# Program order on every engine for the first nine pieces of the first block, and a solve one step sooner, in a fused delta-rule attention and maxout kernel

## The chip, the cores and the metric

The kernel runs on one core of one Trainium2 chip. The metric is the device time of one execution in microseconds (us). Engines are called PE (TensorE), ACT (ScalarE), DVE (VectorE), POOL (GpSimd) and SP (SyncE, which issues most of the DMA here). PSUM is the memory in which the kernel's matmul products land. A *hole* is a stretch in which PE stands idle, and *by hand* means in the order of the program. All times and ratios quoted are of runs in the fast state. "L687" is line 687 of the kernel; the lines of all versions shown here agree up to about line 1015.

## The reference, cut to what matters

```python
# q, k, v: (4, 8, 768, 48), beta: (4, 8, 768)
k_n = k / (norm(k) + 1e-6)
for t in range(768):                       # delta rule, state is 48 x 48 per head
    y[t]  = q[t] @ state
    v_old = state.T @ k_n[t]
    state += beta[t] * outer(k_n[t], v[t] - v_old)
x = y as (3072, 384)
out = max(x @ w1, x @ w2, x @ w3) @ w_out  # d_ff = 768
```

The kernel does the attention in 12 chunks of 64 tokens, two chunks to a group. In each group a triangular system is solved (`solve`, many small DVE instructions), its result is multiplied out by matmuls, and the output of a finished group is the input of one block of the maxout network (`ffn`). The six blocks of `ffn` are the frame of the program: each yields after every piece of matmuls, and between two pieces the program emits a bit of the attention of the next group.

## The kernel before

Products of the attention go through one PSUM tag (a set of buffers under one name) with **three** buffers; the maxout products have two of their own:

```python
def ps_ffn(shape, name):
    return psum.tile(shape, FP32, name=name, tag="ffn", bufs=2)

def ps_two(name):                                   # p_k, p_q, p_g, p_t, p_e, ...
    return psum.tile([128, 2, 512], FP32, name=name, tag="two", bufs=3)
```

Those that the argument follows, and what empties their buffers:

```python
def old_k(c):      # link "k": product p_k, emptied by DVE at L687; needs the scaled v_t
    nc.vector.tensor_tensor(out=rhs, in0=rhs, in1=times_state(kqt, 0, "p_k"), op=ALU.subtract)
def old_q(c):      # link "q": product p_q, emptied by ACT at L695
    nc.scalar.copy(heads(qs), times_state(kqt, 1, "p_q"))
# gram ("P", "g"): product p_g, emptied by DVE at L395 (masked product pt) or ACT at L428 (at)
# turn ("T", "t"): transposes p_t, emptied by ACT at L345 (kqt)
# halves_z ("e"): product p_e, emptied by ACT at L614 (z)
```

Work on the same engines that waits for transfers:

```python
def prep_sums(c):
    for g in range(2):
        nc.scalar.square(ksq, kk)                      # L267, needs the key tile kpad
        nc.vector.tensor_reduce(out=..., in_=ksq, ...) # L268
    for bb in range(2):                                # "flip": halves exchanged by DMA
        nc.sync.dma_start(out=ksum[rows(bb), 1], in_=kflip[rows(1 - bb)])   # L273
def prep_values(c):
    norm(...)         # root on ACT (L245), Newton step on DVE (L246 to L250)
    scale(c, nrm)     # v_t on POOL (L277)
def prep(c): prep_sums(c); prep_values(c)              # cut
def weights():        # one piece a step: mant, up on ACT (L211, L220), POOL, DVE, POOL
    ...               # needs w_bits, a staged DMA
```

The first block and the main loop. Within `manual_schedule` an engine keeps the order of the program; engines outside it are ordered by the scheduler. So before piece 4 all engines follow the program, from there only PE does:

```python
for i, _ in enumerate(ffn(0)):
    if i == 4:                                         # the border
        by_hand.close()
        tc.no_sync_barrier()
        by_hand = ExitStack()
        by_hand.enter_context(tc.manual_schedule(engines={mybir.EngineType.PE}))
    if i > 3:
        some(conv, 1)                                  # one conversion of weights
        fetch(nc.sync)
    queries(FIRST.get(i, ""))
    links(1, EARLY_LINKS.get(i, ""))                   # 9: "k0 q0", 10: "e0 t0", ...
    ...
    if i in (8, 9):
        prep(i - 6)
    ...                                                # cut
# main loop: all engines by hand
for m in range(1, GROUPS):
    for i, _ in enumerate(ffn(m)):
        if i < 2: some(solving, 1)                     # steps below: 3, from piece 18 on 4
        if m + 2 < GROUPS:
            if i == 9:  blocks(m + 2)
            if i == 11: solving = solve(m + 2)
        if i > 11: some(solving, steps - 2)
        links(m + 1, LINKS.get(i, ""))   # "d": T1's transposes, "t": turn, "L", "N": loads
        if i >= 11: some(solving, 2)
```

Of the kernel before, what the change touches and what calls it, by code (L numbers as in the profile page):

```python
# [21 lines left out]
def kernel(  # L22
# [81 lines left out]
    def rows(bb):  # L104
        return slice(C * bb, C * (bb + 1))
# [6 lines left out]
    def load(src, dst, n, queues):  # L112
        c, g = divmod(n, 2)
        for bb in range(2):
            queues[bb].dma_start(
                out=dst[rows(bb ^ g), :, 0:D],
                in_=src[2 * bb + g, :, c * C : (c + 1) * C, :].rearrange(
                    "h p d -> p h d"
                ),
            )  # L120

    def load_k(n, queues=one_queue):
        load(k, kpad[n % NK], n, queues)

    def load_q(n, queues=one_queue):
        load(q, qpad[n % NQ], n, queues)

    def load_v(c):
        vts[c] = work.tile([128, 2, H, D], FP32, name="v_t", bufs=3)
        for bb in range(2):  # L130
            nc.sync.dma_start(
                out=vts[c][rows(bb)].rearrange("p g h d -> p (g h) d"),
                in_=v[2 * bb : 2 * bb + 2, :, c * C : (c + 1) * C, :].rearrange(
                    "b h p d -> p (b h) d"
                ),
            )
# [28 lines left out]
    t1 = [const.tile([128, 2, H, BL], FP32, name=f"t1{i}") for i in range(NU)]  # L165
# [22 lines left out]
    def fetch(queue=nc.scalar):  # L188
        if fetched[0] < len(pieces):
            _, src, (a, b) = pieces[fetched[0]]  # L190
            st = work.tile([128, 2 * 384], U32, name="w_bits", bufs=5)
            queue.dma_start(
                out=st.rearrange("p (a b) -> p a b", a=a), in_=src
            )
            staged.append(st)
            fetched[0] += 1
# [46 lines left out]
    def norm(out, ksum, root, t):  # L243

        nc.scalar.sqrt(root, ksum)  # L245
        nc.vector.tensor_scalar_max(t, root, 1e-30)  # L246
        nc.vector.reciprocal(t, t)
        nc.vector.tensor_tensor(out=t, in0=t, in1=ksum, op=ALU.mult)
        nc.vector.tensor_tensor(out=t, in0=t, in1=root, op=ALU.add)
        nc.vector.tensor_scalar(  # L250
            out=out, in0=t, scalar1=0.5, scalar2=1e-6, op0=ALU.mult, op1=ALU.add
        )

    def small(name, *shape):
        one = name[-1] == "0" or name[-2:] == "bl" or name == "warm"
        return work.tile([128, *shape], FP32, name=name, bufs=2 - one)
# [3 lines left out]
    def prep_sums(c):  # L260


        ksum, kflip = small("ksum", 2, H), small("kflip", H)
        for g in range(2):
            kk = kpad[(2 * c + g) % NK][:, :, 0:D]
            ksq = work.tile([128, H, D], FP32, name="ksq", tag="o_sb")
            nc.scalar.square(ksq, kk)  # L267
            nc.vector.tensor_reduce(  # L268
                out=kflip if g else ksum[:, 0], in_=ksq,
                axis=mybir.AxisListType.X, op=ALU.add,  # L270
            )
        for bb in range(2):
            nc.sync.dma_start(out=ksum[rows(bb), 1], in_=kflip[rows(1 - bb)])  # L273
        sums[c] = ksum

    def scale(c, nrm):
        nc.gpsimd.tensor_tensor(  # L277
            out=vts[c], in0=vts[c],
            in1=nrm[:, :, :, None].to_broadcast([128, 2, H, D]), op=ALU.mult,
        )  # L280

    def prep_values(c):

        nrm = small("nrm", 2, H)
        norm(nrm, sums.pop(c), small("root", 2, H), small("newton", 2, H))
        scale(c, nrm)
# [30 lines left out]
    def prep(c):  # L317
        prep_sums(c)
        prep_values(c)
# [38 lines left out]
    def load_blocks(n):  # L358
        c, g = divmod(n, 2)
        for i in range(2):  # L360
            t = turned[n, i] = work.tile(
                [128, 2, TURNED], FP32, name="turned", tag="w_bits", bufs=5
            )
            nc.gpsimd.memset(t[:, :, TURNED - 48 : TURNED], 0.0)  # L364
            for bb in range(2):
                for par in range(2):
                    for db in range(2):
                        p0, at = DP * par + 32 * db, 32 * (1 - db)
                        (nc.sync, nc.gpsimd)[i].dma_start(  # L369
                            out=t[p0 : p0 + 32, bb, at : at + NP * 2 * D].rearrange(  # L370
                                "p (j x) -> p j x", j=NP
                            ),
                            in_=(k, q)[i][
                                2 * bb + g, :, c * C : (c + 1) * C, :
                            ].rearrange(
                                "(j two) (r tb) d -> two r j (tb d)", two=2, tb=2
                            )[par],
                        )
# [483 lines left out]
    def some(gen, n):  # L862
        for _ in range(n):
            if next(gen, gen) is gen:
                break

    conv = weights()
    solving = solve(0)
# [86 lines left out]
    for n in range(2):  # L955
# [4 lines left out]
    solving = solve(1)  # L960
# [3 lines left out]


    LINKS = {
        0: "k0 q0 t0 L2", 1: "g0 t1 L3", 2: "g1 t2", 3: "d0 d1", 4: "z0", 5: "z1 g2",
        6: "j0 t3", 7: "j1 g3", 8: "u0", 9: "s0", 10: "y0", 11: "k1 q1 x0",
        12: "w0 V0", 13: "u1", 14: "K0 K1 V1", 15: "y1 x1 X0", 16: "K2 K3 p0",
        17: "s1 w1 p1", 18: "N0 P0", 19: "X1 P1", 20: "N1",  # L970
    }
    EARLY_LINKS = {
        9: "k0 q0", 10: "e0 t0", 11: "e1 t1", 12: "f0 g0", 13: "f1 d0 g1",
        14: "z0 d1 t2", 15: "z1 g2", 16: "j0 t3", 17: "j1 g3", 18: "u0", 19: "s0",
        20: "k1 q1", 21: "y0", 22: "u1", 23: "x0", 24: "s1", 26: "y1", 28: "x1",
    }


    FIRST = {
        0: "f1 s0 T2 S1 S1", 1: "z1 d1 S1 k1 P2 T3 S1 S1", 2: "j1 S1 S1 S1",  # L980
        3: "P3 S1 q1 S1 S1", 4: "u1 T4", 5: "y1", 6: "s1 T5 P4", 7: "x1 T6",
        8: "P5 T7", 12: "P6", 14: "P7",
    }


# [8 lines left out]
    def links(m, names):  # L994
        for name in names.split():
            f, i = name[0], int(name[1])
            if f in RECURS and m < GROUPS:
                RECURS[f](2 * m + i)
            elif f in MADE and m + 1 < GROUPS:
                MADE[f](2 * (m + 1) + i)  # L1000
            elif f in UNIT and m + 1 < GROUPS:
                UNIT[f](4 * (m + 1) + i)
            elif f == "N" and m + 2 < GROUPS:
                load_blocks(4 * (m + 2) + i)

    def queries(names):
        for name in names.split():
            f, n = name[0], int(name[1])
            if f not in OF_KEYS:
                links(0, name)  # L1010
                continue
            OF_KEYS[f](n)
            if f == "T" and n + 3 < 11:
                load_q(n + 3)
# [1 line left out]


    for i, _ in enumerate(ffn(0)):
        if i == 4:
            by_hand.close()  # L1020
            tc.no_sync_barrier()
            by_hand = ExitStack()
            by_hand.enter_context(tc.manual_schedule(engines={mybir.EngineType.PE}))
        if i > 3:
            some(conv, 1)
            fetch(nc.sync)
        queries(FIRST.get(i, ""))
        links(1, EARLY_LINKS.get(i, ""))
        if 4 <= i < 8:
            some(solving, 2)  # L1030
        if i == 4:
            load_v(3)
        if 5 <= i < 9:
            load_k(3 + i)
        if i in (8, 9):
            prep(i - 6)
        if i == 12:
            load_q(11)
        if i in (15, 18):
            load_v(4 + i // 18)  # L1040
        if i in (18, 20):
            prep(4 + i // 20)
        if i == 19:
            blocks(2)
        if i == 21:
            solving = solve(2)
            some(solving, 1)
        if 21 <= i < 29:
            some(solving, 4)
        if i in (27, 28):  # L1050
            load_blocks(i - 15)
# [8 lines left out]
    for m in range(1, GROUPS):  # L1060
        for i, _ in enumerate(ffn(m)):
            if i < 2:
                some(solving, 1)
            if m + 2 < GROUPS:
                if i == 9:
                    blocks(m + 2)
                if i == 11:
                    solving = solve(m + 2)
            steps = 4 if i >= 18 else 3
            if i > 11:  # L1070
                some(solving, steps - 2)
            links(m + 1, LINKS.get(i, ""))
            if i >= 11:
                some(solving, 2)
    by_hand.close()
# [28 lines left out]
```

## Time and profile before

| | us |
|---|---|
| median time of 3 runs | 599.53 (595.86 to 600.70) |
| profiled span | 596.8 |
| start of the first p_h | 60.2 |
| first block, up to the first p_h of the next | 134.4 |
| blocks 1 to 5 | 82.2, 88.8, 88.9, 76.1, 66.2 |

The block borders are the starts of the first p_h after a run of p_o. The lines of the page and of the blocks are in the prediction below. One stretch that the prediction did not show turned out to matter. It is from the instructions in order of time (start us, us, engine and line, output and inputs, and in brackets the idle time of the engine before it and what ended that):

```profile
103.41 1.15 PE L675 MATMUL p_k<-st,kqt 48*64 48x48 f32 x64
...
106.60 0.80 ACT L695 COPY qs<-p_q 128x768 f32<-128x768 f32 x1 [1.80 <-PE p_q L675]
...
107.97 1.14 PE L611 MATMUL p_e<-ut,at 64*64 64x32 f32 x64
...
126.71 0.94 DVE L687 TENSOR_TENSOR v_t<-v_t,p_k 128x768 f32<-128x768 f32 x1
```

ACT stood ready for p_q and emptied its buffer at once. p_k, in contrast, kept its buffer for more than 22 us, until L687, and PE went on meanwhile with the other two.

### The profile page before, as it was taken

Reading aid. Unit: us, or ns where it says so; the run is one execution under the profiler, and the core shown is the slowest. Engines: PE = TensorE matmul, PEld = TensorE weight load, DVE = VectorE, ACT = ScalarE, POOL = GpSimd, SP = SyncE. Lnnn points to the kernel's source line nnn. Section 1 sums busy time; section 2 is a strip of 40 time slices with the busy share of each in tenths; the row PEclk is TensorE's granted clock in tenths of the full one; section 3 lists DMA queues with packets and bytes.
Section 4 is the critical chain, followed back from the end, with each engine's and each line's share of the span. In section 5 each row is a group of like instructions: output and inputs, shape, how many; then the busy total and the mean of one; then the engine's idle time right before and its main releaser. Section 6 shows DMA issues by size and latency. Waiting matters only on the chain.

```text
span 596.8 us, 18730 instructions
## 1 busy us (share of the span) xinstructions
PE 547.5 (92%) x8106; PEld 322.4 (54%) x8106; DVE 343.4 (58%) x778; ACT 139.8 (23%) x274; POOL 119.7 (20%) x209
## 2 busy tenths in 40 slices
PE   5467888978999999999979999979999999999997
PEld 4346766765556545555435555545555455554444
DVE  1658886696399463899363899363898422211110
ACT  3336246555111221121111212111211111010000
POOL 6024224258210512005602005600001000000000
PEclk9555698988999999999979999979999999999999
DMA  9999739754701654454734654733653202210002
GB/s 159 162 169 243 147 71 184 192 142 104 121 17 26 145 115 82 98 117 110 170 86 82 116 99 106 178 83 57 121 103 74 42 2 55 61 45 1 0 0 53
DMA packets 159505, 58.76 MB, mean 98 GB/s; under 512 B 141184, under 2 KB 153280, under 8 KB 159424
## 3 DMA queue, kind: packets, MB, share of 16 engines
q1 hardware_dynamic: 150736, 51.58, 41.4%
q0 software_dynamic: 3200, 4.82, 3.6%
q10 hardware_dynamic: 5488, 1.18, 1.2%
q8 instruction: 63, 1.03, 0.8%
q14 instruction: 18, 0.15, 0.1%
HBM read 40.21 MB, written 17.30 MB: 96 GB/s over the span
## 4 chain that ended last, share of the span: by engine, by line
PE 69%; DVE 4%; SPq 2%; issue 1%; DMA 1%; ACT 0%; POOL 0%; DVEq 0%; POOLq 0%; ACTq 0%
PE p_h L822 42%; PE p_o L846 16%; PE p_g L411 2%; PE p_u L703 2%; PE p_y L743 2%; PE p_k L675 2%; PE p_s L725 1%; PE p_q L675 1%; SPq L369 1%; PE p_j L658 1%; DVE tmp L519 1%; DMA turned<-in_k_dram 1%; DVE y_bl L523 1%; SPq L537 0%; DVE h L832 0%
## 5 line engine op out<-in xcount | busy, mean ns | idle before, releaser
L822 PE MATMUL p_h<-xt,w_sb 128*128 128x512 f32 (+1 forms) x702 | 308.2, 585 | 5.8 <-DVE h L832 4.2
L822 PEld LDWEIGHTS p_h<-xt,w_sb 128*128 128x128 f32 x702 | 132.6, 198 | 130.1 <-issue 114.6
L832 DVE TENSOR_TENSOR h<-h,p_h 128x512 f32<-128x512 f32 (+1 forms) x78 | 50.2, 644 | 100.7 <-PE p_h L822 100.4
L846 PE MATMUL p_o<-wo_sb,h 128*128 128x384 f32 x288 | 94.4, 487 | 0.6 <-DVE h L832 0.6
L846 PEld LDWEIGHTS p_o<-wo_sb,h 128*128 128x128 f32 x288 | 54.3, 190 | 38.1 <-issue 1.7
L277 POOL TENSOR_TENSOR v_t<-v_t,nrm 128x768 f32<-128x768 f32 x12 | 17.9, 1491 | 204.0 <-DVE nrm L250 129.9
L523 DVE TENSOR_TENSOR y_bl<-y_bl,tmp 128x31 f32<-128x31 f32 (+20 forms) x139 | 53.3, 384 | 4.7
L369 POOL DMA_DIRECT2D turned<-in_q_dram x96 | 52.2, 551 | 3.1 <-POOL turned L364 3.1
L519 DVE TENSOR_TENSOR tmp<-x_bl,y_bl 128x31 f32<-128x31 f32 (+20 forms) x139 | 47.1, 339 | 4.1
L830 ACT COPY h<-p_h 128x512 f32<-128x512 f32 (+1 forms) x39 | 21.5, 552 | 106.2 <-PE p_h L822 106.2
L411 PE MATMUL p_g<-kqt 48*64 48x64 f32 (+1 forms) x1280 | 34.1, 255 | 11.8 <-ACT kqt L345 7.5
L411 PEld LDWEIGHTS p_g<-kqt 48*64 48x64 f32 x1280 | 28.6, 152 | 20.8 <-ACT kqt L345 9.4
L854 ACT COPY o_sb<-p_o 128x384 f32<-128x384 f32 x24 | 11.4, 477 | 88.5 <-PE p_o L846 80.9
L385 DVE STREAM_TRANSPOSE kqt<-turned 128x256 f32<-128x256 f32 x48 | 17.5, 417 | 20.2 <-DMA turned<-in_k_dram 20.1
L428 ACT COPY at<-p_g 128x512 f32<-128x512 f32 x21 | 12.3, 585 | 55.3 <-DVE pt L395 49.8
L238 POOL TENSOR_TENSOR w_sb<-mant,up 128x384 int32<-128x384 int32 x18 | 18.4, 1026 | 15.8 <-DVE mant L234 14.7
L215 POOL TENSOR_SCALAR mant<-mant 128x384 f32<-128x384 f32 x24 | 12.7, 530 | 44.1 <-ACT mant L211 44.0
L731 DVE TENSOR_TENSOR st<-st,p_s 128x768 f32<-128x768 f32 x11 | 10.4, 950 | 17.5 <-PE p_s L725 17.4
L695 ACT COPY qs<-p_q 128x768 f32<-128x768 f32 x11 | 8.8, 798 | 47.2 <-DVE v_t L687 27.6
L743 PEld LDWEIGHTS p_y<-u,pt 64*64 64x64 f32 x768 | 13.1, 142 | 10.7 <-issue 7.6
L618 DVE TENSOR_SCALAR ut<-p_j 32x512 f32<-32x512 f32 (+1 forms) x13 | 8.3, 647 | 16.7 <-ACT ut L620 16.7
L703 PEld LDWEIGHTS p_u<-v_t,ut 64*64 64x64 f32 x768 | 13.4, 142 | 8.4 <-issue 7.8
(111 smaller groups left out, 496.6 us busy)
## 6 DMA issues: line engine op xcount, KB each, us to landing
w_bits<-in_moe_w_dram SPq DMA_DIRECT2D x18, 384.0 KB
at_d<-at SPq DMA_DIRECT2D x45, 128.0 KB
v_t<-in_v_dram SPq DMA_DIRECT2D x24, 192.0 KB
turned<-in_q_dram POOLq DMA_DIRECT2D x96, 48.0 KB, 3.1
turned<-in_k_dram SPq DMA_DIRECT2D x96, 48.0 KB
out_dram<-o_sb SPq DMA_DIRECT2D x48, 96.0 KB
kpad<-in_k_dram SPq DMA_DIRECT2D x44, 96.0 KB
y_x<-y SPq DMA_DIRECT2D x16, 192.0 KB
```

Source lines behind the costliest of these rows:

```text
L238: nc.gpsimd.tensor_tensor(out=dst.bitcast(I32), in0=mant_v.bitcast(I32), in1=up_v, op=ALU.add)
L369: (nc.sync, nc.gpsimd)[i].dma_start(out=t[p0 : p0 + 32, bb, at : at + NP * 2 * D].rearrange("p (j x) -> p j x", j=NP), in_=(k, q)[i][2 * b ...
L411: nc.tensor.matmul(p_g[rows(bb ^ (g * i)), par, c0 : c0 + C * (1 + whole)], kq[:, 0], kq if whole else kq[:, i],)
L519: nc.vector.tensor_tensor(out=t_v, in0=row.to_broadcast(t_v.shape), in1=column.to_broadcast(t_v.shape), op=ALU.mult,)
L523: nc.vector.tensor_tensor(out=rest, in0=rest, in1=t_v, op=ALU.subtract)
L675: nc.tensor.matmul(p_b[rows(bb), par, c0 : c0 + D], kqt[g][dims(par), j, bb ^ g, i], st[dims(par), bb ^ g, g, j],)
L703: nc.tensor.matmul(p_v[rows(bb ^ g), g, i], ut[c % NU][rows(bb), g, h], rhs[rows(bb), g, h],)
L743: nc.tensor.matmul(p_v[rows(bb), g, i], pt[g][r, h], u[r, g, h])
L822: nc.tensor.matmul(p_h, w_sb[i][:, t, f * 128 : (f + 1) * 128], xt[:, t, lo : lo + w], start=(t == 0), stop=(t == KT - 1),)
L830: nc.scalar.copy(h, p_h)
L832: nc.vector.tensor_tensor(out=h, in0=h, in1=p_h, op=ALU.max)
L846: nc.tensor.matmul(p_o, hs[f][:, i * 128 : (i + 1) * 128], wo_sb[:, f], start=(f == 0), stop=(f == FT - 1),)
```

## The change

The intent, in three parts. A unit is one chunk of two of the four batch entries; T1 is a transposed block of the solve's result. (a) In blocks 1 to 3, T1's transposes ("d") go one chunk at a time and ahead of the transposes of the third unit ("t2"). (b) In the same loop the solve of a later group starts one piece sooner. (c) In the first block all engines follow the program up to piece 8 (the border moves from 4 to 9), and inside the pieces the copies go ahead of the conversions, the sums of chunks 2 and 3 come sooner, and so do two masked products ("P6", "P7", two pieces each).

```diff
-        0: "k0 q0 t0 L2", 1: "g0 t1 L3", 2: "g1 t2", 3: "d0 d1", 4: "z0", 5: "z1 g2",
-        6: "j0 t3", 7: "j1 g3", 8: "u0", 9: "s0", ...
+        0: "k0 q0 t0 L2", 1: "g0 t1 L3", 2: "g1 d0", 3: "z0 d1", 4: "z1 t2",
+        5: "j0 g2", 6: "j1 t3", 7: "u0 g3", 9: "s0", ...
@@ FIRST
-        8: "P5 T7", 12: "P6", 14: "P7",
+        8: "P5 T7", 10: "P6", 12: "P7",
@@ first block
-        if i == 4:
+        if i == 9:
             by_hand.close()
             ...
+        queries(FIRST.get(i, ""))
+        links(1, EARLY_LINKS.get(i, ""))
         if i > 3:
             some(conv, 1)
             fetch(nc.sync)
-        queries(FIRST.get(i, ""))
-        links(1, EARLY_LINKS.get(i, ""))
-        if 4 <= i < 8:
-            some(solving, 2)
         if i == 4:
             load_v(3)
+            some(solving, 4)
-        if 5 <= i < 9:
+        if i in (5, 6):
+            load_k(3 + i)
+            some(solving, 1)
+        if i in (7, 8):
             load_k(3 + i)
+        if i in (5, 6):
+            prep_sums(i - 3)
         if i in (8, 9):
-            prep(i - 6)
+            prep_values(i - 6)
@@ main loop
-                if i == 9:
+                if i == 8:
                     blocks(m + 2)
-                if i == 11:
+                if i == 10:
                     solving = solve(m + 2)
-            if i > 11:
+            if i > 10:
                 some(solving, steps - 2)
             links(m + 1, LINKS.get(i, ""))
-            if i >= 11:
+            if 10 <= i < 20:
                 some(solving, 2)
```

## The prediction

> **What bounds the kernel now.** I read the page first (its busy shares and its forty slices), then busy time by stretch for each later block, then the chain of waits, then the instructions in order of time around every hole on PE.
>
> ```profile
> PE 547.5 (92%) x8106; PEld 322.4 (54%) x8106; DVE 343.4 (58%) x778; ACT 139.8 (23%) x274; POOL 119.7 (20%) x209
> ...
> PE   5467888978999999999979999979999999999997
> ...
> PEclk9555698988999999999979999979999999999999
> ```
>
> PE is the bound. From slice 13 on it is full, but for two sevens, and the granted clock drops in the same two slices. Before slice 12 both rows are ragged. So there are two places to gain: the first maxout block, and two holes later. The chain's row of starts of p_h and p_o gives the block borders 194.6, 276.8, 365.6, 454.5 and 530.6 us. By stretch (busy time and count of PE, PEld, DVE, ACT, POOL; granted clock; DMA share; GB/s):
>
> ```profile
> 194.60:276.80 82.20, 82.20 (x1246) 45.02 (x1245) 55.42 (x125) 15.79 (x30) 15.32 (x30) 1.00 0.53 113
> 276.80:365.60 88.80, 84.78 (x1246) 45.83 (x1244) 59.05 (x134) 15.87 (x30) 21.49 (x42) 0.96 0.53 109
> 365.60:454.50 88.90, 85.15 (x1246) 46.27 (x1246) 60.24 (x139) 15.67 (x30) 16.80 (x32) 0.96 0.50 105
> ```
>
> The three blocks have the same 1246 PE instructions, and the first of them has no hole: 82.2 us is what PE needs. The other two take 88.8 and 88.9. The instructions in order of time in the second (start us, us, engine line):
>
> ```profile
> 284.57 1.19 SPq L528 DMA_DIRECT2D y_d<-y_bl  x2
> ...
> 288.00 5.17 SPq L537 DMA_DIRECT2D ut<-y_d  x8
> ...
> 293.27 4.82 SPq L369 DMA_DIRECT2D turned<-in_k_dram  x8
> ...
> 299.64 1.10 DVE L385 STREAM_TRANSPOSE kqt<-turned 128x256 f32<-128x256 f32 x3 [2.47 <-DMA turned<-in_k_dram]
> ...
> 303.35 0.69 DVE L832 TENSOR_TENSOR h<-h,p_h 128x512 f32<-128x512 f32 x1
> ...
> 304.09 5.07 PE L822 MATMUL p_h<-xt,w_sb 128*128 128x512 f32 x6 [2.20 <-DVE h L832]
> ```
>
> The solve's result goes out late (y_d), the ut loads wait for it on the SP queue, the key tiles of the third unit (L2) are issued behind them, DVE stands at L385 for them, and behind L385 on DVE stand six transposes of T1 (L569, L571) and the maximum L832 that PE needs. PE idles 1.82 + 2.20 = 4.0 us (the first before p_g), and the piece at 304.09 takes 5.07 us where its neighbours take 2.8: 2.2 more; together 6.2 of the 6.6 us. The third block does the same.
>
> The first block's holes (60 to 178 us) are short and many. The largest:
>
> ```profile
> 87.94 1.15 PE L743 MATMUL p_y<-u,pt 64*64 64x48 f32 x64 [2.42 <-ACT u L708]
> ...
> 96.63 1.36 PE L757 MATMUL p_x<-ident,y 128*128 128x128 f32 x6 [2.13 <-ACT kqt L345]
> ...
> 127.71 1.12 PE L339 MATMUL p_t<-ident,kpad 128*128 128x128 f32 x4 [1.66 <-DVE v_t L687]
> ...
> 141.27 2.00 PE L411 MATMUL p_g<-kqt 48*64 48x64 f32 x64 [1.74 <-ACT kqt L345]
> ```
>
> With .83, .71, .58, .61 and .81 us more I add 11.5 us of PE waiting from 84 to 142 us, and some 4 us in which matmuls of 128x256 run at the lower clock after it.
>
> **What the Trainium skill says.** "Perfetto Trace Analysis", Per-engine timelines: ACT, DVE and GpSimd are strict FIFO. The trace agrees: a ready maximum (its piece ended by 294.5) ran at 303.35, behind L385. "TensorE: Matmul & The Clock Gate", Part 1: the clock falls to half after an idle window of about 3.4 us and returns after as long a busy one. Agrees in kind: after 4 us of holes one piece ran 5.07 for 2.8 us and the next 2.8 again. "DMA: Bandwidth & Descriptors", Issuing engines are not separate DMA queues: issuing time is usually small beside the DMA. Here it is not: eight issues take 4.8 to 5.2 us on SP, while issue to landing is 3.1 us at the median for these tiles.
>
> **The change, part by part.** No instruction is added or removed on PE; it is all order. I compared the two orders on every engine.
>
> (a) Blocks 1 to 3, order on DVE. T1's transposes of chunk 0, the copy of z0, T1 of chunk 1 and the maximum now stand before the four transposes of the third unit (t2), which moves from piece 2 to piece 4; its gram moves from piece 5 (beside z1) to piece 5 (beside j0), and g3 goes behind u0. The number of bursts between the maxout pieces stays, so PE's 82.2 us stays. What goes: in the frame of block 2, p_z1 ends near 296.2, its copy by 297.6 (0.69), so DVE reaches t2 at 297.6 instead of 290.0. L2's tiles landed by 299.64 in the old order, so even unmoved only 2.0 us are waited, and the gram is wanted at 299.7.
>
> (b) Solve one piece sooner. Its setup starts after y0 (DVE free at 238.2) rather than after k1 (242.2): 4.0 us. The maximum (0.69) and L687 (0.95) that went before it now come inside, and DVE is packed from there to 281.3, so the end moves by 4.0 - 1.6 = 2.4 us, to 278.9. y_d also comes ahead of the last N1 loads and the last output pair on SP, so it is issued at 279.0 instead of 284.6. Then N1's eight issues (4.7), two outputs (1.1), the eight ut (5.2) and L2: 279.0 + 1.2 + 4.7 + 1.1 + 5.2 = 291.2 against 293.3. Landing (6.4 us after the first issue in block 2) at 297.6: just when DVE comes. By this both holes close. Gain 2 x 6.6 = 13.2. I take off 1.7: N1 lands some 1.5 us later, and its transposes and g1 in the next piece have under 1 us to spare, in three blocks. Net 11.5.
>
> (c) First block. For pieces 4 to 8 all engines follow the program. On ACT the copy of u and both kqt copies now go before the conversions (L211, L220), which waited for POOL's w_sb (2.98 us at 86.6). That removes the holes of 2.42 and 2.13 and about half a microsecond of slow clock: 5. prep_sums moves to pieces 5 and 6, so the norm for v_t of chunk 2, and with it L687, comes long before 126.7: 1.66 less and part of the slow clock behind it, say 2.5. Against it: in the new order ACT squares the keys of four later tiles (L267) directly behind each other, before the copy of z (L614), and DVE reduces them ahead of two maxima. In the old order these tiles were issued on SP at 90.6, 100.7, 104.8 and 109.3, and SP still has some thirty issues of 0.6 us to make before the fourth. If ACT reaches the fourth square near 105 and the tile lands near 111.5, ACT and DVE stand 6 us and PE loses most of what it won. I take off 3.5. Net 4.
>
> Sum: 599.5 - 11.5 - 4 = 584.0.
>
> **Rivals.**
> R1, a new wait in blocks 1 to 3: x_bl is loaded at piece 8 and used at piece 10. For: g3 now stands behind u0, so the at_d writes and the four x_bl issues (228.4 to 233.1 before) come about 1 us later, to end near 234, and in the first block x_bl was used 9 us after its last issue; DVE wants it near 239. Against: other loads land in 2.1 to 5.6 us, and PE has two buffers of slack. Cost if true: 1 to 2 us a block, so 587 to 590.
> R2, the late key squares of (c) are as bad as feared and more: PE loses the 5 us again and idles anew. Then the first block gains nothing or loses 3: 588 to 591.
> R3, the first block gains nearly all of its holes and their slow clock, since the tiles come sooner in a queue that runs ahead: 10 rather than 4, and the later holes close with nothing left: 599.5 - 13.2 - 10 = 576.
> R4, the holes are only moved: T1 of chunk 0 waits at DVE for ut (landing near 290) with the maximum behind it. Against: DVE comes to it near 290 and piece 3 ends at 292. Cost under 1 us.
>
> **Range and chances.** The 13.2 us are nearly mechanical: same work, one block without a hole as the proof. I give 9 to 13 for them. The first block is a matter of interleaving that I cannot see: -3 to +10. That gives 576 to 593.5 at the extremes; I take 575 to 592 for 8 in 10. Faster by over 2% means under 587.5; with a centre of 584 and a spread of about 6, 0.71. Slower by over 2% would need new holes of 25 us: 0.02. Before itself moved between 595.9 and 600.7 us over three runs.
>
> **What would show it.** (a) and (b) are right if the blocks that began at 276.8 and 365.6 both take 82 to 84 us with a granted clock of 1.00, the forty slices lose both sevens, and L385 no longer leads a wait of 6 us. y_d should be issued before the last eight L369, and ut end some 2 us sooner against the block's border. If those blocks still take 86 or more, (b) is wrong: I should see DVE standing at L385, at T1 or at the first step of the solve. (c) is right if the p_y and p_x waits are gone, L687 runs within a few us of its p_k (23 us after it before), and the distance from the first p_h (60.2) to the block border (194.6 before, 134.4 us) is near 130. A wait of ACT at L267 for kpad of some 6 us, with z and the maxima behind it, would show R2; its absence with 125 us for the block would show R3. The prediction is wrong as a whole if the stages before 60 us, whose order is unchanged, move by more than 1 us, or if the last two blocks (76.1 and 66.2 us) change by more than that.

## The result, and the profile after

The changed kernel took **606.11 us** (605.14 to 607.95, 4 runs) beside 598.75 (595.86 to 600.70, 4 runs) for the kernel before. The ratio is 1.0131, with a 95% interval of 1.0081 to 1.0180. A ratio here is the mean time of one kernel's fast runs over the mean of the other's fast runs in the same rounds, so it is not quite the ratio of the medians. It is slower by 1.3%; 584.0 was expected.

From the page of the changed kernel (forty slices of its span):

```profile
PE   7468698376999999999999999999999999999997
...
PEclk9656789587899999999999999999999999999999
```

From slice 12 on both rows are full: the two sevens of before are gone. The loss must lie before. By stretch, blocks 1 to 3 (span, then busy time and count of PE, PEld, DVE, ACT, POOL; granted clock; DMA share; GB/s):

```profile
209.17:292.15 82.98, 82.30 (x1246) 44.82 (x1245) 57.30 (x132) 15.92 (x30) 15.65 (x31) 1.00 0.49 107
292.15:376.90 84.75, 82.94 (x1246) 45.30 (x1245) 58.92 (x133) 15.92 (x30) 21.34 (x42) 1.00 0.54 115
376.90:462.00 85.10, 82.99 (x1245) 45.31 (x1244) 60.17 (x139) 15.93 (x30) 16.95 (x33) 1.00 0.52 109
```

| stage, us | before | after | difference |
|---|---|---|---|
| up to the first p_h | 60.2 | 61.9 | +1.7 |
| first block | 134.4 | 147.3 | **+12.9** |
| blocks 1 to 3 | 259.9 | 252.8 | -7.1 |
| blocks 4 and 5 | 142.3 | 142.4 | +0.1 |

The stage up to the first p_h has the same order in both. In the profiles of all the versions it ends between 60.2 and 62.8 us, so I take its 1.7 us as spread, though the prediction had called more than 1 us there a sign against itself. The first block lost what the later ones gained and more. The instructions in order of time show where (changed kernel):

```profile
99.55 1.15 PE L675 MATMUL p_k<-st,kqt 48*64 48x48 f32 x64
...
100.52 1.39 PE L675 MATMUL p_q<-st,kqt 48*64 48x48 f32 x64
...
103.33 0.69 PE L411 MATMUL p_g<-kqt 48*64 48x64 f32 x32
...
109.60 0.22 ACT L245 ACTIVATE root<-ksum 128x16 f32<-128x16 f32 x1 [6.14 <-DMA ksum<-kflip]
...
111.34 0.94 DVE L687 TENSOR_TENSOR v_t<-v_t,p_k 128x768 f32<-128x768 f32 x1
...
112.34 2.03 PE L611 MATMUL p_e<-ut,at 64*64 64x32 f32 x64 [8.31 <-DVE v_t L687]
...
115.55 0.52 ACT L267 ACTIVATE ksq<-kpad 128x384 f32<-128x384 f32 x1 [4.03 <-DMA kpad<-in_k_dram]
...
116.85 0.79 ACT L695 COPY qs<-p_q 128x768 f32<-128x768 f32 x1
...
117.69 1.11 PE L339 MATMUL p_t<-ident,kpad 128*128 128x128 f32 x4 [3.32 <-ACT qs L695]
...
123.42 1.59 PE L611 MATMUL p_e<-ut,at 64*64 64x32 f32 x64 [1.89 <-DVE pt L395]
```

PE had finished p_g by 104.0 us and then stood 8.3 us for L687, ran p_e at about half speed (2.03 us; 1.14 before), and stood 3.3 us more for qs and 1.9 for L395: one after another, the three instructions that empty p_k, p_q and p_g released it. Until p_e it had been ahead: it was ready for p_e 42.1 us after the first p_h, where it began p_e 47.8 us after it before. So 5.6 us had been won, and 18.5 were lost from there to the border. (Later holes add to those shown, the longest 3.7 us before a p_g at 138.6.) ACT stood for the second flip (6.1 us) and for a late key tile (4.0 us); the copy qs, whose product was ready at 101.9, ran at 116.85. On DVE, L687 stood behind the first Newton step of the second norm, for which DVE waited 4.4 us, until ACT had its root.

The third product, p_g, is P6, which the change itself had moved ahead of p_e. That move is not the cause on its own: in e17 below P6 is in its old place, and PE stands 18.9 us one product later, before p_t, until L687 frees a buffer.

### The profile page after: what moved, and what is told of

Read it like the earlier page. It is cut to its first block, busy times and chain, and to the rows that moved or that the text cites. A ratio compares the mean times of both kernels' runs of the same rounds, so it can differ in the third digit from the quotient of the medians.

```text
span 604.4 us, 18708 instructions
## 1 busy us (share of the span) xinstructions
PE 547.6 (91%) x8106; PEld 324.1 (54%) x8106; DVE 346.4 (57%) x778; ACT 140.6 (23%) x274; POOL 119.5 (20%) x209
## 4 chain that ended last, share of the span: by engine, by line
PE 67%; DVE 13%; DMA 8%; SPq 3%; ACT 3%; issue 3%; POOL 2%; ACTq 0%; DVEq 0%; POOLq 0%
PE p_h L822 41%; PE p_o L846 10%; PE p_g L411 4%; DMA kpad<-in_k_dram 3%; DVE y_bl L523 3%; DVE tmp L519 2%; PE p_u L703 2%; PE p_t L339 2%; PE p_k L675 1%; DMA ksum<-kflip 1%; PE p_y L743 1%; SPq L115 1%; PE p_j L658 1%; PE p_s L725 1%; PE p_q L675 1%
## 5 line engine op out<-in xcount | busy, mean ns | idle before, releaser
L822 PEld LDWEIGHTS p_h<-xt,w_sb 128*128 128x128 f32 x702 | 131.0, 196 | 126.0 <-issue 111.2
L523 DVE TENSOR_TENSOR y_bl<-y_bl,tmp 128x31 f32<-128x31 f32 (+20 forms) x139 | 55.0, 395 | 4.7
L411 PE MATMUL p_g<-kqt 48*64 48x64 f32 (+1 forms) x1280 | 35.2, 260 | 12.9 <-ACT kqt L345 4.9
L411 PEld LDWEIGHTS p_g<-kqt 48*64 48x64 f32 x1280 | 29.9, 158 | 22.0 <-issue 8.7
L854 ACT COPY o_sb<-p_o 128x384 f32<-128x384 f32 x24 | 11.5, 479 | 87.4 <-PE p_o L846 83.4
L215 POOL TENSOR_SCALAR mant<-mant 128x384 f32<-128x384 f32 x24 | 12.9, 535 | 49.9 <-ACT mant L211 49.8
L395 DVE TENSOR_TENSOR pt<-p_g,mask 128x512 f32<-128x512 f32 x22 | 15.2, 690 | 7.7 <-PE p_g L411 7.4
L230 DVE TENSOR_SCALAR mant<-mant 128x384 uint32<-128x384 uint32 x24 | 15.4, 641 | 6.1 <-POOL mant L215 5.9
L339 PE MATMUL p_t<-ident,kpad 128*128 128x128 f32 x48 | 10.9, 378 | 8.6 <-DMA kpad<-in_k_dram 4.2
L364 POOL MEMSET turned<- 128x96 f32 x24 | 4.0, 186 | 73.5 <-DVE kqt L385 71.8
```

The lines of the kernel that those rows point to most:

```text
L339: nc.tensor.transpose(p_t[:, i, j * 128 : (j + 1) * 128], src[:, 2 * j : 2 * j + 2], ident,)
L411: nc.tensor.matmul(p_g[rows(bb ^ (g * i)), par, c0 : c0 + C * (1 + whole)], kq[:, 0], kq if whole else kq[:, i],)
L523: nc.vector.tensor_tensor(out=rest, in0=rest, in1=t_v, op=ALU.subtract)
L822: nc.tensor.matmul(p_h, w_sb[i][:, t, f * 128 : (f + 1) * 128], xt[:, t, lo : lo + w], start=(t == 0), stop=(t == KT - 1),)
```

## The experiments

Seventeen kernels ran, in five groups; each group shared its runs of the kernel before (medians 599.05, 598.88, 599.34, 597.92, 598.67 us). All were correct. One single run each of e1, e5, e7, e8 and e10 was of the slow state; ratios and medians are without it. The groups ran on different chips, so across groups the ratios are the better comparison. "First block" is from one profile each. The same first block in two kernels differed by up to 3.5 us between profiles (124.2 and 127.7 in the last two of the table), so smaller differences of it prove nothing.

| run | edit against the changed kernel | median us | ratio to before (95%) | first block us |
|---|---|---|---|---|
| before | | 597.9 to 599.5 | 1 | 134.4 |
| changed | | 606.11 | 1.0131 (1.0081 to 1.0180) | 147.3 |
| e1_blocks_only | first block as before | 593.30 | 0.9892 (0.9839 to 0.9945) | 134.1 |
| e2_first_only | main loop as before | 613.63 | 1.0232 (1.0179 to 1.0285) | 148.5 |
| e3_sums_early | both sums at piece 4 | 607.11 | 1.0138 (1.0105 to 1.0171) | 147.7 |
| e4_no_hoist | second border at 18 | 603.30 | 1.0058 (1.0024 to 1.0092) | 142.3 |
| e5_both | e3 and e4 | 602.09 | 1.0070 (1.0047 to 1.0093) | 140.5 |
| e6_border4 | border at 4 | 592.60 | 0.9910 (0.9884 to 0.9936) | 134.0 |
| e7_border11 | border at 11 | 599.51 | 1.0001 (0.9979 to 1.0024) | 137.8 |
| e8_border11_sums | border at 11, sums at 4 | 600.94 | 1.0037 (1.0015 to 1.0059) | 143.4 |
| e9_act_hand | from 9 ACT by hand too | 594.51 | 0.9917 (0.9895 to 0.9938) | 136.5 |
| e10_dve_hand | from 9 DVE by hand too | 598.91 | 0.9998 (0.9965 to 1.0031) | 139.5 |
| e11_border18 | border at 18 | 589.39 | 0.9839 (0.9786 to 0.9892) | 129.0 |
| e12_border5 | border at 5 | 592.37 | 0.9892 (0.9838 to 0.9945) | 133.4 |
| e13_n1_sooner | e11, loads N1 sooner | **582.13** | **0.9718** (0.9674 to 0.9763) | 127.6 |
| e16_old_pieces18 | old pieces, border at 18 | 603.08 | 1.0088 (1.0046 to 1.0131) | 144.1 |
| e17_old_pieces9 | old pieces, border at 9 | 613.70 | 1.0254 (1.0221 to 1.0287) | 152.4 |
| e14_late_third | e11, third chunk later | 588.09 | 0.9824 (0.9774 to 0.9874) | 124.2 |
| e15_n1_late3 | e13 and e14 | 582.87 | 0.9756 (0.9703 to 0.9809) | 127.7 |

### Which half of the change: e1 and e2

```diff
# e1_blocks_only: kernel before, with the change's LINKS and main loop alone
# e2_first_only: kernel before, with the change's FIRST and first block alone
```

> The kernel before with the change in blocks 1 to 5 alone (new table of links, solve one piece sooner); the first block as before. If the two parts add up, the later blocks are worth what the trace of the changed kernel shows: blocks 2 and 3 at 84.75 us in place of 88.8 and 88.9, block 1 at 83.0 in place of 82.2, so 598.75 - 8.2 + 0.8 = 591.4 us. Rival: the later blocks only look good because the first one is late (its transfers have had more time), then 595 or more.

> The changed kernel with the old links and the old solve in blocks 1 to 5: the change in the first block alone. If the two parts add up: 606.1 + 8.2 - 0.8 = 613.5 us, and the distance from the first p_h to the border of the first block stays near 147 us (134.4 before). Rival, that the parts interact: 608 or less.

Measured 0.9892 and 1.0232. Their differences from 1 add up to +1.2%, and the whole change measured +1.3%: within intervals of about half a per cent the two halves add up. e2 came out as expected for that (613.6 us, 613.5 expected); e1's 593.3 us lie between the 591.4 of that case and the 595 of its rival. The main loop gains; the first block alone loses 13.9 us in time (1.0232 of the 599 of before).

### Two single causes: e3 and e4

The first theories took the two waits of ACT at their word. A: the second flip is issued too late. B: the scheduler, which orders ACT and DVE from piece 9 on, has pulled the squares of four late key tiles ahead of qs.

```diff
# e3_sums_early
         if i == 4:
             load_v(3)
             some(solving, 4)
+            prep_sums(2)
+            prep_sums(3)
         ...
-        if i in (5, 6):
-            prep_sums(i - 3)
# e4_no_hoist
-        if i == 9:
+        if i in (9, 18):
```

> The changed kernel, but the squares, sums and flips of chunks 2 and 3 both at piece 4, ahead of the ut and key loads on SP. Theory A (the second flip lands at 109.5 behind eight ut loads, ACT stands 6.1 us at its square root, DVE at the norm, and L687 behind it frees p_k's bank late): the hole of 8.3 us before p_e goes, some 8 us less, 598. Theory B (the squares of four late key tiles, moved up by the scheduler, hold ACT and DVE): PE only waits a little later, 604 to 606. Theory C (program order in pieces 4 to 8 makes the weights late): 605 to 606.

> The changed kernel with a second scheduling border at piece 18, so that the squares of the last two chunks (keys 8 to 11) cannot move up to piece 9. Theory A: the 8.3 us before p_e stay, and at most 2 us are won. Theory B: ACT's waits for key tiles (4.0 and 1.95 us) go, with the 3.3 us before p_t and the 1.9 us before the second p_e: 600 to 601. Theory C: no change, 606.

Neither cured it: 607.1 and 603.3 us; what e4 won, 2.8 us, is more than A allowed and less than B expected. In e3 the root did not wait any more, but (ACT in order of time):

```profile
110.59 0.52 ACT L267 ACTIVATE ksq<-kpad 128x384 f32<-128x384 f32 x1 [5.53 <-DMA kpad<-in_k_dram]
...
118.74 0.78 ACT L695 COPY qs<-p_q 128x768 f32<-128x768 f32 x1
```

Another square between these two waited 5.5 us. The hole before p_e fell from 8.3 to 3.9 us and the one before p_t rose from 3.3 to 7.5. In e4 the squares were gone from there; ACT then stood 6.3 us at the second root and 3.8 us at a conversion, and the holes were 10.2 and 4.7. Whatever I took away, ACT stood for the next transfer, and qs stood behind it.

### A third theory: e5 to e8

D: when PE comes to p_e, the products p_k, p_q and p_g hold all three buffers of the tag, and the three instructions that empty them were placed behind work that waits for transfers. What has to change is the order, not the transfer. Its rivals: A and B together, and C, that program order in pieces 4 to 8 makes loads and weights late and is itself the fault.

```diff
# e5_both: e3_sums_early and e4_no_hoist together
# e6_border4
-        if i == 9:
+        if i == 4:
# e7_border11
-        if i == 9:
+        if i == 11:
# e8_border11_sums: e7 with prep_sums(2) and prep_sums(3) at piece 4, as in e3
```

> Both single cures together: the two sums of chunks 2 and 3 taken at piece 4 and a second scheduling border at piece 18. The first two runs each moved the wait instead of removing it. New theory D: at about 104 us TensorE has the three products p_k, p_q and p_g in the three PSUM buffers of the tag that p_e needs, and their three evacuations (the subtraction at L687 on VectorE, the copy qs at L695 on ScalarE, the masked product at L395 on VectorE) were placed by the scheduler behind conversions, roots and squares that wait for transfers. Here qs still stands behind five conversions. D: the sum of the holes before the first p_e and the next p_t stays over 8 us (11.6 in the changed kernel, 11.3 and 14.9 in the two cures) and the time is 600 to 608. Theories A and B together (late flips, and squares of late key tiles, are the whole cause): both holes are under 1 us each and the time is 591 to 597.

> The changed kernel with the by-hand order of the first block ended at piece 4, as before; all its moves inside the pieces stay. The build puts qs directly after the evacuation of p_h, ahead of the first root and of the conversions, and L687 ahead of the second root's Newton step. C (program order in pieces 4 to 8 makes weights and loads late) and D (order of the three evacuations) both expect the holes before p_e and p_t to fall under 2 us each; first block 130 to 137 us instead of 147.3, time 588 to 596. If the moves inside the pieces (loads, sums, conversions after the copies) are the cause instead, the first block stays over 142 and the time over 600.

> The changed kernel with the by-hand order continued to piece 10 instead of ending with piece 8. The build shows what moves: on ScalarE the copy qs stands ahead of the two conversions and the second root, and the squares of the late key tiles behind the copies of p_e; on VectorE L687 stands ahead of the second Newton step. D: the wait for qs (3.3 us before p_t) goes, L687 comes at 105 to 107 (after the scaling of v_t at 103.5 to 105.0) instead of 111.3, so the hole before p_e falls from 8.3 to under 4 us; the first block is 134 to 140 us, the time 592 to 599. C (the program order of pieces 4 to 8 is what makes things late): more program order cannot help, the holes before p_e and p_t together stay over 9 us, time 603 to 612.

> As the run with the border at piece 11, with the sums of chunks 2 and 3 taken at piece 4, so that neither root waits for its flip. D: the holes before p_e and p_t are under 3 and under 1 us; time within 3 us of the run with the border at 11 alone, or lower if the second root's wait there delays the mask of p_g. C: no better than the changed kernel, 603 to 612. A (late flip matters once the order is right): at least 3 us faster than the border at 11 alone.

e5 refutes A and B together: 602.1 us, holes of 7.7 and 6.2. The roots ran without a wait; ACT stood 4.6, 5.3 and 3.1 us at three conversions for their w_bits, and qs behind them. e6 cures the block entirely (134.0 us, 592.6), as C and D both expected. e7 recovers 9.5 of the 12.9 us that the first block had lost, and e8 3.9; C allowed neither time. e7's 599.5 us lies just over the range of D. What e7 still loses looks like the same fault one product later: qs and L687 come early, but copies of z stand behind the second root (5.7 us) and a conversion (4.0 us), and PE stands 2.2 and 2.4 us for them. e8 was not faster than e7 (600.9 us), so an earlier flip was no gain there. e6 in order of time:

```profile
103.47 0.80 ACT L695 COPY qs<-p_q 128x768 f32<-128x768 f32 x1 [1.67 <-PE p_q L675]
...
105.34 1.09 PE L611 MATMUL p_e<-ut,at 64*64 64x32 f32 x64
...
111.39 0.95 DVE L687 TENSOR_TENSOR v_t<-v_t,p_k 128x768 f32<-128x768 f32 x1 [1.59 <-POOL v_t L277]
```

L687 ran at 111.39, as late as in the changed kernel (111.34), and PE did not wait for it at p_e. Here one buffer held long cost no wait at p_e; the changed kernel held all of them.

### Which engine's order: e9 to e12

```diff
# e9_act_hand (e10_dve_hand: the same with EngineType.DVE)
-            by_hand.enter_context(tc.manual_schedule(engines={mybir.EngineType.PE}))
+            by_hand.enter_context(tc.manual_schedule(
+                engines={mybir.EngineType.PE, mybir.EngineType.Activation}))
# e11_border18
-        if i == 9:
+        if i == 18:
# e12_border5
-        if i == 9:
+        if i == 5:
```

The built programs show what moves. ACT's instructions in order, in the changed kernel and with the border at 18, from the first root (h is the copy of a maxout product):

```
changed:    root h mant up root ksq ksq mant up ksq mant up qs ksq mant up ...
border 18:  root h qs mant up root z kqt mant up z kqt mant up ...
```

> The changed kernel, border at piece 9 as it is, but from there ScalarE too keeps program order (the change leaves only TensorE by hand). The build shows the copy qs ahead of the conversions and of the second root, the squares of the late key tiles far behind, and VectorE's L687 ahead of the second Newton step, although VectorE is still left to the scheduler. D (the three evacuations p_k, p_q, p_g behind work that waits for transfers): the 3.3 us before p_t for qs go, the hole before p_e falls from 8.3 to under 3 us, first block 133 to 140, time 591 to 599. C (by-hand order of pieces 4 to 8 makes weights and loads late): 603 to 611.

> The changed kernel, but from piece 9 on VectorE too keeps program order, ScalarE stays with the scheduler: L687 stands ahead of the second Newton step, qs on ScalarE behind one conversion, the second root and two squares of late key tiles. D: the hole before p_e for L687 falls under 3 us, but TensorE then waits for qs, 4 to 9 us before p_t or p_e; the two holes together 6 to 10 us (11.6 in the changed kernel), time 598 to 605: half a cure. If only VectorE's order mattered: 590 to 597.

> The changed kernel with every engine by hand through piece 17. qs comes in its place, L687 ahead of the second Newton step, but ScalarE's copy z of the first p_e stands behind the second root (piece 9), which waits for its flip until 109 us or so. D: no wait for L687 over 2 us, none for qs; instead a wait of 2 to 6 us for z (L614) or the mask; first block 134 to 142, time 593 to 601. C: worse than the changed kernel, over 606.

> The changed kernel with the by-hand order ended one piece later than in the run with the border at piece 4 (which was 592.6 us): the copy of u in piece 4 is then ahead of that piece's conversion, so the 2.4 us hole before p_y should go, while from piece 5 the scheduler orders the rest; qs comes after the first root and one conversion, L687 ahead of the second Newton step. D: first block 130 to 135, time 588 to 594. If any by-hand order past piece 4 costs (C): over 596.

e9 falls in D's range (594.5). In order of time:

```profile
102.99 0.80 ACT L695 COPY qs<-p_q 128x768 f32<-128x768 f32 x1
...
106.88 2.03 PE L611 MATMUL p_e<-ut,at 64*64 64x32 f32 x64 [2.78 <-DVE v_t L687]
...
109.83 0.22 ACT L245 ACTIVATE root<-ksum 128x16 f32<-128x16 f32 x1 [5.14 <-DMA ksum<-kflip]
```

The border is still at 9 and the second root still waits 5.1 us, but qs is ahead of it; L687 came early too (105.88), although the scheduler still ordered DVE. e10 is about the half cure that D expected: 598.9 us, with holes of 1.9 and 4.0 (6 to 10 together had been expected). In order of time:

```profile
101.14 0.95 DVE L687 TENSOR_TENSOR v_t<-v_t,p_k 128x768 f32<-128x768 f32 x1 [1.59 <-POOL v_t L277]
...
106.14 0.22 ACT L245 ACTIVATE root<-ksum 128x16 f32<-128x16 f32 x1 [6.56 <-DMA ksum<-kflip]
...
107.08 0.78 ACT L695 COPY qs<-p_q 128x768 f32<-128x768 f32 x1
...
107.92 1.12 PE L339 MATMUL p_t<-ident,kpad 128*128 128x128 f32 x4 [3.98 <-ACT qs L695]
```

L687 comes early; qs stands behind the root, and PE waits for qs. e11 does better than either kernel, 589.4 us, below the 593 to 601 that D expected, and refutes C: the most program order of all gives the shortest first block so far. Its lines:

```profile
102.31 0.80 ACT L695 COPY qs<-p_q 128x768 f32<-128x768 f32 x1
...
103.16 1.23 PE L611 MATMUL p_e<-ut,at 64*64 64x32 f32 x64
...
104.86 0.95 DVE L687 TENSOR_TENSOR v_t<-v_t,p_k 128x768 f32<-128x768 f32 x1 [1.59 <-POOL v_t L277]
...
105.87 0.66 PE L339 MATMUL p_t<-ident,kpad 128*128 128x128 f32 x4 [1.48 <-DVE v_t L687]
...
108.82 0.22 ACT L245 ACTIVATE root<-ksum 128x16 f32<-128x16 f32 x1 [4.81 <-DMA ksum<-kflip]
```

ACT still stands 4.8 us for the second flip, until 108.8 (until 109.6 in the changed kernel). What PE needs first is no longer behind it: qs had run at 102.3. The wait is nearly the same, and PE no longer stands for it; the wait for z that I had expected in its place was 0.65 us on the weight loads and none on PE. e12 was as expected in time (592.4); the hole before p_y went, but one of 3.4 us came before a p_g, for DVE's y at L745.

### The parts apart, and a better version: e13 to e17

Open were the moves inside the pieces (do they matter?), the second flip (does it still cost anything?), and why blocks 1 to 3 had gained 7.1 us and not 11.5. For the last, block 2 of the changed kernel in order of time:

```profile
294.48 1.09 SPq L528 DMA_DIRECT2D y_d<-y_bl  x2
...
295.92 5.11 SPq L369 DMA_DIRECT2D turned<-in_k_dram  x8
...
302.65 0.45 DVE L385 STREAM_TRANSPOSE kqt<-turned 128x256 f32<-128x256 f32 x1 [1.19 <-DMA turned<-in_k_dram]
```

SP holds the eight issues of N1 (turned) behind y_d, which waits for the solve, and DVE then waits for the tiles.

```diff
# e13_n1_sooner (on e11_border18)
-        17: "s1 w1 p1", 18: "N0 P0", 19: "X1 P1", 20: "N1",
+        17: "s1 w1 p1", 18: "N0 P0", 19: "N1 X1 P1",
# e14_late_third (on e11_border18)
-        if i in (5, 6):
-            prep_sums(i - 3)
-        if i in (8, 9):
-            prep_values(i - 6)
+        if i in (5, 11):
+            prep_sums(2 + i // 11)
+        if i in (8, 14):
+            prep_values(2 + i // 14)
# e15_n1_late3: e13 and e14 together
# e16_old_pieces18, e17_old_pieces9: e1_blocks_only (pieces of the first block as before), with
-        if i == 4:
+        if i == 18:      # e17: 9
```

> The run with the border at piece 18 (589.4 us), with the loads N1 of the second unit put in the head of piece 19 of the main loop, so that on the DMA queue they go ahead of the solve's y_d, not behind it. It tests what took 4.6 us of the expected gain in blocks 1 to 3: theory N1 (the tiles issued behind y_d land too late for VectorE's transposes at L385): the holes before p_g in blocks 2 and 3 (1.1 to 1.7 us each) and the slower piece behind them go, these blocks take 83 us instead of 84.8 to 86.9, time 584 to 588. Rival: y_d then goes out later behind the eight issues, T1's loads are late and a hole of the same size opens a piece later: 588 to 591.

> The run with the border at piece 18, with the sums of chunk 3 moved from piece 6 to 11 and its norm from piece 9 to 14: ScalarE's second root no longer stands in program order between qs and the copies z. If the wait for the second flip still costs something there (theory A in what is left of it): first block 2 to 3 us shorter than 129.0, time 585 to 588. If not (its holes are now under 1.5 us each): within 1.5 us of 589.4, or worse where the moved squares meet T1's work.

> The main loop of the change with the first block's pieces as before (conversions ahead of the copies, sums whole at pieces 8 and 9, P6 and P7 late), but every engine by hand through piece 17. It parts the moves inside the pieces from the by-hand order. Theory M (the moves are needed for by-hand order to gain: conversions would otherwise stand ahead of u and kqt): first block 133 to 140 us, time 593 to 600. Rival (by-hand order alone gives the gain, the moves nothing): within 2 us of the border at 18 with the moves, 588 to 592.

> As before this one, but with the border at piece 9 where the change has it: the border alone, without the moves inside the pieces. The build puts qs behind four conversions and the squares of four key tiles, as in the changed kernel. D: the border at 9 alone loses what the changed kernel loses, holes for L687 or qs of over 6 us together after 100 us, first block over 142, time 601 to 610. Rival (it takes the moves and the border together): 592 to 599.

> The two single steps that each helped the version with the border at piece 18, together: the loads N1 one piece sooner (ratio 0.9718 alone) and the third chunk's sums and norm later (first block 124.2 instead of 129.0 us, ratio 0.9824 alone). They touch different stages, so they should add: first block 124 to 126, blocks 1 to 3 at 83 us each, time 577 to 581, ratio 0.963 to 0.971. If they interfere (the first block then feeds the later ones at another point): 581 to 585.

e13 confirms the N1 theory: 582.1 us (584 to 588 had been expected), and block 1 takes 83.05 us. Blocks 2 and 3 by stretch (same columns as before) are

```profile
272.23:355.28 83.05, 82.37 (x1246) 44.88 (x1245) 59.39 (x134) 15.93 (x30) 21.06 (x42) 1.00 0.56 117
355.28:438.26 82.98, 82.31 (x1246) 44.82 (x1245) 60.35 (x139) 15.82 (x30) 13.20 (x24) 1.00 0.54 111
```

The holes before p_g are gone from them, and the time is below both kernels; at a ratio of 0.9718 it is the only version here that is clearly faster by more than 2%.

e14 is within 1.5 us of e11 in time. Its first block was 124.2 us, but the same first block in e15 took 127.7, and e15 was not faster than e13 (582.9 and 582.1, intervals overlapping): the two steps did not add, as I had expected them to. That the third chunk's preparation costs anything where it stood is not shown.

e16 and e17 show that the moves inside the pieces matter, and more than I had expected: both were slower than their ranges. With the old pieces the sums come at pieces 8 and 9, so under program order the first root waits for its flip even longer. In e16:

```profile
117.27 0.22 ACT L245 ACTIVATE root<-ksum 128x16 f32<-128x16 f32 x1 [17.97 <-DMA ksum<-kflip]
...
119.37 0.90 PE L339 MATMUL p_t<-ident,kpad 128*128 128x128 f32 x3 [11.88 <-ACT qs L695]
```

This puts theory A in its place: here a late flip cost time when something that PE needed was behind it in the queue. (e16 and e17 undo all the moves inside the pieces at once, so which of them counts is not shown.) With the border at 4, where the scheduler orders the rest, the moves are worth nothing (134.0 us with them in e6, 134.1 without in e1). With the border at 18 they are worth some 15 us (129.0 and 144.1); with the border at 9 some 5 (147.3 and 152.4).

## Why the prediction was wrong

**Steps (a) and (b), right in mechanism, too large.** y_d went out 2.3 us after the start of block 2 (7.8 before; 2.2 expected). The clock of the three blocks is 1.00, both sevens are gone, and the last two blocks did not move. The blocks that the prediction wanted at 82 to 84 us took 84.8 and 85.1. The term "I take off 1.7" for N1 was mis-sized: blocks 1 to 3 took 252.8 us, 6.2 more than three times the 82.2 of an undisturbed block. e13 shows what it was. With N1's issues ahead of y_d, they took 249.1, so 3.7 of the 6.2 us were N1, in blocks 2 and 3 (beside e11, the run that e13 edits, it is 6.1: 255.2 against 249.1). So y_d ahead of N1, which the prediction counted as a gain and as a sign of being right, was itself what had to be undone. The rest, some 2.5 us, goes mostly with a hole of 0.68 us in each block ahead of a p_h, for ACT's copy of h; no run tried to remove it. The gain was 7.1 us, against 11.5, and 10.8 with N1 mended.

**Step (c), the term that failed.** "That removes the holes of 2.42 and 2.13 and about half a microsecond of slow clock: 5" came true: both waits are gone and PE was 5.6 us ahead when it reached p_e. "L687 ... comes long before 126.7" came true in the letter (111.34) and was worth nothing by itself: in e6 L687 runs at the same time, and the block takes 134.0 us, as before. It was not "within a few us of its p_k" (11.8 us). The failing term is "I take off 3.5", the price of ACT standing at the late key squares, the only wait that the prediction charged against (c). They stood 6 us in all, as I had estimated (4.03 and 1.95), but from p_e to the border 18.5 us were lost. That is the price of all that stood ahead of qs and L687, and of what followed from it, not of the squares alone: without their waits (e4) 2.8 us came back.

Two things were missing in that term. I had asked which *later* work would be delayed (the copies z and the maxima) and not what was already waiting to be emptied: the order showed qs behind those squares, and p_q's buffer with it. And I had looked at the squares alone. e3, e4 and e5 show that flips, key tiles and weights were interchangeable there; each takes the place of the one removed. R2 named the right kind of loss, with z and the maxima behind the squares where qs was, and put it at 588 to 591; the size was not right.

**Two readings that were wrong.** The prediction sets eight issues (4.8 to 5.2 us) beside one landing of 3.1 us and says that issuing is not small; one issue is about 0.6 us, and the profile page gives the 3.1 us for query tiles, issued by POOL, and no landing time for the key tiles on SP. Its "4 us of holes" before the slow piece are two holes, 1.8 and 2.2 us, with a p_g between them.

**What was shown and what was not.** Shown: the loss lies in the first block (e1, e2), depends on the position of the border (e6, e11), and goes when ACT's and DVE's emptying instructions come before the waiting work (e9, e11), even though the wait for the flip stays (4.8 us in e11). Program order on DVE alone cures about half (e10). That all three buffers are held follows from the code and from who released PE in the traces; a run with a fourth buffer, which would test it directly, was not made. Not shown: why the scheduler, started at piece 9, puts qs behind three conversions, the second root and three squares when, started at piece 4, it does not; and whether the backlog of the DMA queue (SP was at an issue, or at the wait of one, at all times from 88.2 to 124.0 us in the changed kernel) could be shortened instead.

## What to carry to other kernels

When work is re-ordered on an engine that takes its instructions in order, list first the instructions that empty the accumulators of the bounding engine, count how many buffers there are, and look what stands ahead of each. Here PE stood 8.3 and 3.3 us when waits of 6.1 and 4.0 us were ahead of them, and no longer stood for a wait of 4.8 us that was behind them (e11). If removing the wait that the profile names only brings up the next one, move what stands behind it instead. And look what the scheduler is handed at the end of a region under program order: here the same moves lost 13 us with the border at piece 9 and gained 5 with it at 18.

## What the Trainium skill lacked or had wrong

- "PSUM — Partial Sum Buffer", Summary: rules for kernel authors, advises to evacuate promptly. What it lacks is which product may wait: one held for over 22 us (p_k before, 104.6 to 126.7) let PE run on, while with all three buffers held PE stood 8.3 and 3.3 us.
- "Perfetto Trace Analysis", Optimization Strategy, says to find what blocks the gap and make that dependency start sooner or end faster. For what released PE itself this held: with qs and L687 brought forward the time was 589.4 us (e11). What it lacks is the case where that instruction stands behind others that wait: speeding the transfer that they waited for gave 607.1 us against 606.1 (e3).
- "DMA: Bandwidth & Descriptors", Issuing engines are not separate DMA queues, calls the issuing time usually small beside the transfer. What it lacks is that issues add up on one engine and that the later ones stand behind an earlier wait: eight took 5.1 us behind one that waited for DVE, and putting them ahead of it made blocks 1 to 3 shorter by 6.1 us (e13 beside e11).
